# Which queue sends the key bits: seven dictionary and set entries of a hash-attention and SwiGLU kernel

## The chip, the cores and the metric

The kernel runs on one core of a Trainium2 chip. The metric is the device time of one execution in microseconds. Before the change three executions took 327.55, 328.31 and 328.44 us, a median of 328.31 us. One more execution was profiled; the views quoted below are of that one.

## The reference, cut to what matters

The first stage is attention over buckets: six sign bits of a projection give every query and key a bucket number, and a query sees only the keys of its own bucket. The second stage is a SwiGLU layer with RMS norm over the rows that the attention gives.

```
B, H, S, D = 4, 8, 768, 64                      # q, k, v; proj is 64 x 6
q_bits = einsum(q, proj) > 0 ; k_bits = einsum(k, proj) > 0
mask   = bucket(q_bits) == bucket(k_bits)       # bucket = sum of bits * 2^i
attn   = softmax(where(mask, q k^T / 8, -1e9))  # divided by (sum + 1e-9)
x      = (attn v) as 3072 rows of 512
xn     = x / sqrt(mean(x^2) + 1e-6) * rms_g
out    = (silu(xn w_gate) * (xn w_val)) w_out   # 512 -> 1536 -> 512
```

## The kernel before, in words

**Units and steps.** The work is cut into eight units. Unit `u` is one half (384) of the query rows of batch `u // 2`, for all eight heads. A unit has `NS` = 24 steps, three for each head, and a step handles 256 of the 768 keys. The main loop (L916 to L921) does for every step `t`: the scores of step `t + 1` on PE (`scores`, L359), the exponential of step `t` on ACT (`probs`, L371), and then what `plan[t]` holds, in the order in which it was put there with `at(0, t, ...)`. The order of each engine and of each DMA queue is thus written out by hand; nothing reorders it later. Each queue issues in order, and an issue that must wait holds all that stand behind it.

**Bits in the operands.** For each pair of heads `hp` of batch `b` a tile of `qks` (six of them, used in turn, L80) holds q and k transposed in its rows 0 to 63. Rows 64 to 69 hold the six bits as fp16 values of equal size and either sign, so that one matmul gives q k^T plus a large bonus for a full match. For the pairs of `spots` (L714) the bits come about so: `hash_one` projects on PE (L222) when the step in `spots[..][3]` comes, `hash_bits` takes the signs on DVE (L231), and `send_bits` (L306, issue at L312) carries them to the rows of the operand tile with four small DMAs for each head (two for k, two for q; 4.5 KB each). `SENDS` (L809) gives the step of a head's four DMAs where it differs from the hash step; `ONPOOL` (L812) names the heads whose DMAs are issued from GpSimd's queue (POOL) and not from SyncE's (SP). `place` (L814) puts both into a list `late`, which is put into the plan behind everything that the units themselves planned (L884).

**Loads.** `spots` also says at which step a pair's raw q and k blocks are loaded (`load_blocks`, L116: four DMAs for q, four for k, in runs of 128 bytes) and its values (`load_v`, L107: one DMA of 384 KB, or two of 192 KB for pairs in `VSPLIT`, L105). For pair (2, 0) the entry is a triple: k blocks, q blocks, values. All loads share the eight buffers of `lpool` and go out on SP. `turn_dve` transposes blocks on DVE (L192, L199), `cast_pool` writes them into the operand tile from POOL (L212), `v_prep` and `v_sum` copy and sum the values on POOL (L321, L328 to L330).

**A unit's second stage.** While unit `u + 1` does its attention, unit `u` goes through norm and feed-forward. At step 4 of that stretch `norm` (L457) runs: DVE adds up the squares (L422, L450), POOL takes the power -1/2 (`rstd`, L454), DVE scales the rows (`xn`, L463 and L471). One step later `turn_dma` (L439) transposes the 128-row thirds named by `ONDMA` with DMA transposes from SP (L442): two thirds in units 1 to 4 and 6, three in unit 5, one in unit 7. The other thirds go through PE, with the result taken up by DVE (L478, L484). During steps 0 to some 8 PE finishes the output projection of the unit before (`project`, L524; `store`, L534, copies on ACT at L536 and stores 256 KB from SP at L537, one step later than the last matmul). The gate and value matmuls (L495, `g_ps` and `v_ps`) follow and need all thirds of `xnT`.

The places that the change touches are thus steps 53 and 54 (norm and transposes of unit 1), steps 62 (loads), and steps 97 to 101 (norm of unit 3 at step 100, transposes at 101).

Of the kernel before, what the change touches and what calls it, by code (L numbers as in the profile page):

```python
# [33 lines left out]
def kernel(  # L34
# [67 lines left out]
        )  # L102


    VSPLIT = {(2, 3), (3, 0), (3, 1), (3, 2), (3, 3)}  # L105

    def load_v(eng, b, hp):  # L107
        vn = lpool.tile([128, 2, 6, D], FP32, name="vn", tag="L")
        for hs in (slice(0, 1), slice(1, 2)) if (b, hp) in VSPLIT else (slice(0, 2),):
            eng.dma_start(  # L110
# [587 lines left out]
    for hp, ts in ((0, (8, 22, 23, 24, 25, 24, 39, 27, 28, 42)), (1, (20, 26, 28, 29, 30, 29, 41, 32, 33, 43))):  # L698
# [15 lines left out]
    spots = {  # L714
# [91 lines left out]
            inserts[2 * b * NS + s] = (MEAN, v_mean, b, hp, 4)  # L806


    SENDS = {(1, 2, 0): 54, (1, 2, 1): 54, (2, 0, 0): 77, (2, 0, 1): 77, (2, 2, 1): 101, (3, 2, 1): 149}  # L809


    ONPOOL = {(1, 2, 0), (1, 2, 1)}  # L812

    def place(t, step):  # L814
        if step[0] is None:
# [2 lines left out]
        if step[0] is hash_one:  # L818
            late.append((t, hash_bits, *step[1:]))
            for pair in step[1:]:  # L820
                for hh in range(2):
                    s = SENDS.get((*pair, hh), t)
                    eng = nc.gpsimd if (*pair, hh) in ONPOOL else nc.sync
                    late.append((max(s, t), send_bits, *pair, hh, eng))
# [150 lines left out]
```

## Time and profile before

| what | us |
|---|---|
| three runs: lowest, median, highest | 327.55, 328.31, 328.44 |
| the profiled execution's own time | 328.73 |
| its span, first to last instruction | 326.9 |
| PE busy, of the span | 320.4 |
| VectorE (DVE) / ScalarE (ACT) / GpSimd (POOL) busy | 227.5 / 228.4 / 160.4 |
| granted TensorE clock | 1.000 |

Times in the views count from the start of the span. A row of the timeline gives start, duration, engine, line of the kernel, instruction, result and operands, how many were merged into the row (x4), and in square brackets how long the engine had been idle before it and who released it. "SPq" is the queue of SyncE, on which most DMAs are issued: the duration there is that of issuing, not of the transfer. "PEld" is TensorE's weight load.

### The profile page before, as it was taken

The numbers are of one execution on the slowest core, as the hardware profiler recorded it, in microseconds if no ns is written. First come the engines' busy times: TensorE is split into PE (matmuls) and PEld (weight loads), VectorE is DVE, ScalarE is ACT, GpSimd is POOL, SyncE is SP. The second block draws the span as 40 slices with busy tenths as digits, with TensorE's granted clock in tenths as the row PEclk, the third lists the DMA queues.
The fourth block names the chain that finished last, engine by engine and source line by source line (L and its number), as shares of the span: only waits on it lengthen the run. The fifth ranks groups of instructions, "written<-read, shape, count | busy, mean of one in ns | idle before, by whom it ended". The sixth has DMA issues, their size and how long they took to land.

```text
span 326.9 us, 7765 instructions
## 1 busy us (share of the span) xinstructions
PE 320.4 (98%) x2943; PEld 194.0 (59%) x2943; DVE 227.5 (70%) x510; ACT 228.4 (70%) x333; POOL 160.4 (49%) x211
## 2 busy tenths in 40 slices
PE   9999999999999999999899999999999999999996
PEld 4576666655566565655466556665656556665554
DVE  5887876866888568874689558787567536773870
ACT  6899987677678676777667768686777768754322
POOL 3999849957967363731873522742582111221000
PEclk9999999999999999999999999999999999999999
DMA  7953999984728863056547047001300040002002
GB/s 231 357 173 91 223 214 199 172 172 82 167 35 158 153 141 87 7 90 127 108 110 146 34 106 138 7 6 52 99 6 3 1 99 32 2 2 96 17 2 96
DMA packets 87613, 33.03 MB, mean 101 GB/s; under 512 B 72780, under 2 KB 84504, under 8 KB 87576
## 3 DMA queue, kind: packets, MB, share of 16 engines
q1 hardware_dynamic: 83416, 27.71, 36.3%
q0 software_dynamic: 3936, 4.76, 8.7%
q8 instruction: 23, 0.38, 0.5%
q14 instruction: 14, 0.11, 0.1%
q10 hardware_dynamic: 224, 0.07, 0.1%
HBM read 28.58 MB, written 6.29 MB: 107 GB/s over the span
## 4 chain that ended last, share of the span: by engine, by line
PE 94%; DMA 2%; DVE 1%; ACT 1%; SPq 0%; issue 0%; POOL 0%
PE g_ps L495 19%; PE v_ps L495 19%; PE s_ps L359 19%; PE y_ps L524 16%; PE o_ps L384 10%; PE t_ps L160 2%; PE d_ps L222 2%; DMA xnT<-xn 2%; PE d_ps L242 2%; PE z_ps L591 1%; PE y_ps L543 1%; ACT psb L371 1%; PE x_ps L478 1%; PE m_ps L343 1%; SPq L442 0%; DVE xn L463 0%
## 5 line engine op out<-in xcount | busy, mean ns | idle before, releaser
L371 ACT ACTIVATE psb<-s_ps,ebias 128x768 f16<-128x768 f32 x192 | 167.9, 900 | 18.3 <-PE s_ps L359 17.1
L359 PE MATMUL s_ps<-QK 128*128 128x384 f16 (+1 forms) x384 | 93.5, 326 | 1.2 <-ACT psb L371 1.1
L503 ACT ACTIVATE t<-g_ps 128x384 f32<-128x384 f32 x96 | 47.2, 492 | 55.6 <-PE g_ps L495 53.4
L495 PE MATMUL g_ps<-xnT,wg 128*128 128x384 f16 x384 | 82.5, 326 | 1.8 <-DMA xnT<-xn 1.7
L495 PE MATMUL v_ps<-xnT,wv 128*128 128x384 f16 x384 | 82.0, 326 | 0.0
L512 DVE SCALAR_TENSOR_TENSOR a<-t,g_ps 128x384 f32<-128x384 f32 x96 | 52.9, 551 | 33.1 <-ACT t L503 31.6
L406 POOL TENSOR_TENSOR x<-otmp,rcp 128x384 f32<-128x384 f32 x29 | 24.3, 838 | 91.3 <-DVE rcp L404 91.1
L524 PE MATMUL y_ps<-wo,ht 128*128 128x512 f16 x276 | 67.5, 379 | 0.0
L513 DVE SCALAR_TENSOR_TENSOR ht<-a,v_ps 128x384 f16<-128x384 f32 x96 | 53.2, 554 | 11.5 <-PE v_ps L495 3.6
L384 PEld LDWEIGHTS <-psb 128*128 128x128 f16 x1152 | 52.0, 97 | 15.1 <-issue 0.6
L384 PE MATMUL o_ps<-vl,psb 128*128 128x65 f16 x1152 | 55.8, 193 | 0.0
L359 PEld LDWEIGHTS <-QK 128*128 128x128 f16 (+1 forms) x384 | 34.7, 98 | 33.8 <-issue 8.6
L495 PEld LDWEIGHTS <-wg 128*128 128x128 f16 x384 | 35.1, 97 | 23.5 <-issue 2.7
L495 PEld LDWEIGHTS <-wv 128*128 128x128 f16 x384 | 35.1, 97 | 20.8 <-issue 0.2
L524 PEld LDWEIGHTS <-ht 128*128 128x128 f16 x276 | 24.9, 98 | 23.2
L399 DVE TENSOR_TENSOR otmp<-o_ps,cvb 128x390 f32<-128x390 f32 x32 | 17.8, 557 | 9.2 <-PE o_ps L384 9.2
L536 ACT COPY ysb<-y_ps 128x512 f32<-128x512 f32 x23 | 13.5, 587 | 15.0 <-PE y_ps L524 15.0
L412 POOL TENSOR_TENSOR sq<-x 128x384 f32<-128x384 f32 x24 | 19.9, 827 | 1.9
L212 POOL CAST QK<-qT 64x768 f16<-64x768 f32 x20 | 16.4, 821 | 8.3 <-DVE qT L199 7.6
L212 POOL CAST QK<-kT 64x768 f16<-64x768 f32 x20 | 16.4, 821 | 7.7 <-DVE kT L199 5.7
L199 DVE STREAM_TRANSPOSE kT<-kL 128x192 f32<-128x192 f32 x32 | 16.6, 520 | 0.0
L199 DVE STREAM_TRANSPOSE qT<-qL 128x192 f32<-128x192 f32 x32 | 16.1, 523 | 0.0
(86 smaller groups left out, 268.1 us busy)
## 6 DMA issues: line engine op xcount, KB each, us to landing
out_dram<-ysb SPq DMA_DIRECT2D x23, 256.0 KB
vn<-in_v_dram SPq DMA_DIRECT2D x11, 384.0 KB
qL<-in_q_dram SPq DMA_DIRECT2D x40, 96.0 KB
kL<-in_k_dram SPq DMA_DIRECT2D x40, 96.0 KB
kn<-in_k_dram SPq DMA_DIRECT2D x5, 384.0 KB
qn<-in_q_dram SPq DMA_DIRECT2D x5, 384.0 KB
vn<-in_v_dram SPq DMA_DIRECT2D x10, 192.0 KB
wg<-in_moe_w_gate_dram POOLq DMA_DIRECT2D x2, 768.0 KB, 8.8
```

Of the source, the lines that this page charges most:

```text
L199: nc.vector.transpose(dst.rearrange("p (c t r) -> p r c t", c=6, r=4)[:, r], src.rearrange("p (r c) d -> p r c d", r=4)[:, r],)
L212: nc.gpsimd.tensor_copy(QK[b, 2 * hp + hh, "h"][0:64, o : o + S], src[64 * hh : 64 * hh + 64, :])
L359: nc.tensor.matmul(ps[:, j, 0:HALF], QK[b, h, "h"][rows, S + jt * 128 : S + (jt + 1) * 128], QK[b, h, "h"][rows, half * HALF : (half + 1) ...
L371: nc.scalar.activation(psb[u, h][:, 2 * ch : 2 * ch + 2, :], sps.pop((u, i))[:, :, 0:HALF], AF.Exp, bias=ebias, scale=ESCALE,)
L384: nc.tensor.matmul(o[:, c, hh, 0:65], psb[u, h][:, jt, c * 128 : (c + 1) * 128], vls[b % 2][:, h, 2 * (jt % 3) + jt // 3 if b in PARITY el ...
L406: eng.tensor_mul(xd.rearrange("p c (h d) -> p c h d", h=2), tmp[:, :, :, 0:64], r.to_broadcast([128, 3, 2, 64]),)
L412: eng.tensor_mul(sq, xd, xd)
L495: nc.tensor.matmul(ps, w[:, kt, fs], xnT[u][:, kt, :], start=(kt == 0), stop=(kt == 3))
L503: nc.scalar.activation(t, fbank[u, ft, "g_ps"], AF.Tanh, scale=0.5)
L512: nc.vector.scalar_tensor_tensor(out=a, in0=t, scalar=1.0, in1=g, op0=ALU.add, op1=ALU.mult)
L513: nc.vector.scalar_tensor_tensor(out=ht[u][:, ft, :], in0=a, scalar=0.5, in1=vv, op0=ALU.mult, op1=ALU.mult)
L524: nc.tensor.matmul(y, ht[u][:, ft, c * 128 : (c + 1) * 128], wo[:, ft, :], start=(ft == 0), stop=(ft == NF - 1),)
```

## The change

Seven entries change; no function does.

- `VSPLIT` keeps only pair (3, 3): the values of (2, 3), (3, 0), (3, 1) and (3, 2) are loaded by one DMA each and no longer by two.
- Pair (2, 0): its k and q blocks are loaded at step 54 (before: 53), and its values at step 62 (before: 54).
- Batch 1's third pair, second head (1, 2, 1): its four bit DMAs go out at step 53 on SP, behind the transposing DMAs of unit 1. Before they went out at step 54 on POOL, behind those of the first head, which stay there.
- Batch 2's third pair (2, 2): the bit DMAs of both heads go out on POOL at step 101, behind the power of unit 3's norm. Before they went out on SP: those of the first head at step 97, ahead of unit 3's transposing DMAs, and those of the second at step 101, behind them.

```diff
-    VSPLIT = {(2, 3), (3, 0), (3, 1), (3, 2), (3, 3)}
+    VSPLIT = {(3, 3)}
...
-        (2, 0): ((53, 53, 54), (63, 64, 65, 66), (67, 69, 70, 71), 73),
+        (2, 0): ((54, 54, 62), (63, 64, 65, 66), (67, 69, 70, 71), 73),
...
-    SENDS = {(1, 2, 0): 54, (1, 2, 1): 54, (2, 0, 0): 77, (2, 0, 1): 77, (2, 2, 1): 101, (3, 2, 1): 149}
+    SENDS = {(1, 2, 0): 54, (1, 2, 1): 53, (2, 0, 0): 77, (2, 0, 1): 77, (2, 2, 0): 101, (2, 2, 1): 101, (3, 2, 1): 149}
...
-    ONPOOL = {(1, 2, 0), (1, 2, 1)}
+    ONPOOL = {(1, 2, 0), (2, 2, 0), (2, 2, 1)}
```

The instructions of PE, DVE and ACT and their order are the same in both kernels. SP's queue around unit 1 reads after the change: transposes x2, bits of (1, 2, 1) x4, a store, k blocks x4, q blocks x4, a store, bits of (1, 3) x8, values of (2, 0), blocks of (2, 1). Before it read: transposes x2, k blocks x4, q blocks x4, a store, values of (2, 0), a store, bits of (1, 3) x8, blocks of (2, 1). Around unit 3 it reads after the change: values of (3, 0), a store, transposes x2, a store, blocks of (3, 1). Before: values of (3, 0) x2, bits x4, a store, transposes x2, bits x4, a store, blocks of (3, 1).

## Prediction

> **What bounds the kernel now.** I read the page's busy line first, then PE's waits, then PE's timeline where it waits, and last SP's queue in front of those places.
>
> ```profile
> PE 320.4 (98%) x2943; PEld 194.0 (59%) x2943; DVE 227.5 (70%) x510; ACT 228.4 (70%) x333; POOL 160.4 (49%) x211
> PE g_ps L495 <- DMA xnT<-xn: 1.7, 2, 1.5
> PE s_ps L359 <- ACT psb L371: 1.1, 2, 0.8
> 79.51 0.48 PE L495 MATMUL g_ps<-xnT,wg 128*128 128x384 f16 x2 [0.27 <-DMA xnT<-xn]
> 153.94 1.03 PE L524 MATMUL y_ps<-wo,ht 128*128 128x512 f16 x4
> 156.44 0.48 PE L495 MATMUL g_ps<-xnT,wg 128*128 128x384 f16 x2 [1.47 <-DMA xnT<-xn]
> ```
>
> PE is busy in 320.4 of 326.9 us, and the change leaves its instructions as they are. So it can win only what PE waits, and lose by new waits. PE waits twice for the DMA transposes: 0.27 us before unit 1's first gate matmul and 1.47 us before unit 3's. Together 1.74 us; that is all there is to win, since the change touches nothing that ACT's two waits hang on. The row at 153.94 says when PE ran out of work: 153.94 + 1.03 = 154.97, and 156.44 - 1.47 says the same.
>
> Now what holds the transposes, on SP, DVE and ACT:
>
> ```profile
> 74.22 1.42 DVE L463 SCALAR_TENSOR_TENSOR xn<-x,rstd,grow 128x512 f16<-128x512 f32 x2 [1.00 <-POOL rstd L454]
> 75.00 2.63 SPq L442 DMA_TRANSPOSE xnT<-xn  x2
> ...
> 146.22 1.06 SPq L110 DMA_DIRECT2D vn<-in_v_dram  x2
> 147.38 3.03 SPq L312 DMA_DIRECT2D QK<-bits  x4
> 150.52 0.38 SPq L537 DMA_DIRECT2D out_dram<-ysb  x1
> 151.00 2.59 SPq L442 DMA_TRANSPOSE xnT<-xn  x2
> 146.45 0.59 ACT L536 COPY ysb<-y_ps 128x512 f32<-128x512 f32 x1 [1.10 <-PE y_ps L524]
> 148.57 1.41 DVE L463 SCALAR_TENSOR_TENSOR xn<-x,rstd,grow 128x512 f16<-128x512 f32 x2 [0.97 <-POOL rstd L454]
> ```
>
> In unit 1 SP is idle and issues the first transpose 75.00 - 74.22 = 0.78 us after DVE has begun on `xn`: the data sets the time. In unit 3 it is 151.00 - 148.57 = 2.43 us. There SP is the one that is late: four bit DMAs (3.03 us, 0.76 each) and a store lie ahead.
>
> **Unit 3, part by part.** The four bit DMAs go from ahead of the transposes to POOL. The values need one issue and not two; one takes 0.59 us (row at 107.91, below), so SP is free at 146.81. The store's data is ready when ACT's copy ends, 146.45 + 0.59 = 147.04; its 0.38 us ends by about 147.5, before `xn` exists. So the first transpose goes out at 148.57 + 0.78 = 149.35, 1.65 us earlier. How long from there to the matmul? Four units show it:
>
> ```profile
> 111.06 3.71 SPq L442 DMA_TRANSPOSE xnT<-xn  x2
> 116.39 0.49 PE L495 MATMUL g_ps<-xnT,wg 128*128 128x384 f16 x2
> 117.36 0.81 PE L495 MATMUL v_ps<-xnT,wv 128*128 128x384 f16 x4
> 189.70 2.57 SPq L442 DMA_TRANSPOSE xnT<-xn  x2
> 193.64 0.81 PE L495 MATMUL g_ps<-xnT,wg 128*128 128x384 f16 x4
> ```
>
> Unit 1: 79.51 - 75.00 = 4.51, PE waiting. Unit 3: 156.44 - 151.00 = 5.44, PE waiting. Units 2 and 4 didn't wait, so the data was there in at most 5.33 and 3.94. Unit 1 is the nearest, since eight of POOL's bit DMAs ran beside it, as they will now in unit 3. 149.35 + 4.51 = 153.86; with the worst, 149.35 + 5.44 = 154.79. Both are before 154.97. So the whole 1.47 us goes, with 1.1 to 0.2 us of cover left. What is late next: `v_ps` needs the bank that ACT's copy of the last `y_ps` frees, at 155.01 + 0.59 = 155.60 (row below); unit 2 shows `v_ps` 0.97 us behind `g_ps`, so it is due at 155.94. No wait.
>
> **The bits on POOL.**
>
> ```profile
> 73.30 0.88 POOL L454 TENSOR_TENSOR rstd<-ss,mhalf 128x3 f32<-128x3 f32 x1 [1.71 <-DVE ss L450]
> 74.15 4.09 POOL L312 DMA_DIRECT2D QK<-bits  x8
> 147.68 0.86 POOL L454 TENSOR_TENSOR rstd<-ss,mhalf 128x3 f32<-128x3 f32 x1 [1.04 <-DVE ss L450]
> 155.01 0.83 POOL L406 TENSOR_TENSOR x<-otmp,rcp 128x384 f32<-128x384 f32 x1 [6.48 <-DVE rcp L404]
> QK<-bits POOLq DMA_DIRECT2D x8, 4.5 KB, 1.9
> 155.01 0.59 ACT L536 COPY ysb<-y_ps 128x512 f32<-128x512 f32 x1 [0.17 <-PE y_ps L524]
> 158.38 0.49 PE L359 MATMUL s_ps<-QK 128*128 128x384 f16 x2
> 159.96 0.49 PE L359 MATMUL s_ps<-QK 128*128 128x384 f16 x2
> ```
>
> Eight issues took 4.09 us (0.51 each) in unit 1. In unit 3 they start behind the power, 147.68 + 0.86 = 148.54, and end at 152.63. Queued behind them on POOL is L406, which waits for DVE until 155.01: 2.4 us of cover. With 1.9 us from issue to landing the first head's bits are there at 148.54 + 2.05 + 1.9 = 152.5, the second's at 154.5. Their readers are the scores of unit 4's heads 4 and 5: the first is step 108, 159.96 now and 158.49 after the gain, the second three steps of about 1.6 us later. 6 us of cover; cost zero. DVE's `xn` took 1.42 us beside POOL's issues and 1.41 without them, so DVE isn't slowed.
>
> Here a page speaks against the change. The Trainium skill, "SBUF — State Buffer", section "SBUF: two separate sides", says that a DMA issued from GpSimd can't get its descriptors written while VectorE runs in a mode that takes both ports; its part "A bandwidth-pool intuition that's wrong (but worth ruling out)" gives about 620 ns alone and 3100 ns beside such an operation. By it eight issues could take some 20 us (an estimate from that page's ratio), and the change would lose. The trace of unit 1, 0.51 us each beside `xn`, doesn't bear this out.
>
> **Unit 1.** Four of POOL's eight bit DMAs leave; the four that stay end at 74.15 + 2.05 = 76.2, before the second transpose is issued (L442's second half, about 76.4). So unit 1 comes near unit 4, which had none: 75.00 + 3.94 = 78.94 at the latest, against 79.51 - 0.27 = 79.24 where PE needs it. I take the full 0.27; the bounds are 0 and 0.27.
>
> What moves on SP behind the transposes:
>
> ```profile
> 77.72 2.69 SPq L125 DMA_DIRECT2D kL<-in_k_dram  x4
> 88.86 6.00 SPq L312 DMA_DIRECT2D QK<-bits  x8
> 97.67 3.65 SPq L125 DMA_DIRECT2D kL<-in_k_dram  x4
> 107.91 0.59 SPq L110 DMA_DIRECT2D vn<-in_v_dram  x1
> 108.75 0.37 SPq L537 DMA_DIRECT2D out_dram<-ysb  x1
> 88.03 0.50 PE L359 MATMUL s_ps<-QK 128*128 128x384 f16 x2
> 91.26 0.53 DVE L199 STREAM_TRANSPOSE kT<-kL 128x192 f32<-128x192 f32 x1
> 105.40 0.51 DVE L199 STREAM_TRANSPOSE kT<-kL 128x192 f32<-128x192 f32 x1
> 118.28 0.83 POOL L321 CAST vl<-vn 128x768 f16<-128x768 f32 x1
> 100.00:101.00 1.00, 1.00 (x8) 0.59 (x6) 0.86 (x4) 0.66 (x2) 0.48 (x1) 1.00 0.21 31
> 110.00:112.00 2.00, 2.00 (x19) 1.10 (x18) 1.76 (x3) 1.38 (x2) 0.21 (x1) 1.00 0.83 298
> ```
>
> Four bit issues (6.00 / 8 = 0.75 each, 3.0 us) and one store (0.4) come ahead of pair (2, 0)'s blocks. The bits are issued by 80.7 and land by 82.6; unit 2's head 5 reads them at 88.03. The k blocks go out 3.5 us later, by 83.9, the q blocks by 86.7, the last store by 87.1; DVE first turns k at 91.26. Pair (1, 3)'s bits wait for DVE until 88.86 as before, with 1.7 us of room on SP. The values of (2, 0) now follow those bits and are read at 118.28. All hidden.
>
> They push the blocks of (2, 1) and (2, 2), though, by one issue, 0.59 us: the k blocks of (2, 1) are issued by 101.9 for a turn at 105.40; unit 2's store ends on SP at 109.7, and its transposes start at 111.06, still set by DVE. On SP this costs nothing. On the DMA engines 384 KB more have to go through between 95 and 112 us; the slice at 100 has a share of 0.21 only, so most of it fits. I take zero; the upper bound is the transfer itself, 384 KB (393,216 bytes) at the 298 GB/s of the last row, 1.3 us, all of it in front of unit 2's transposes.
>
> **The single value loads** save SP 1.06 - 0.59 = 0.47 us four times. Nothing reads half of such a load, and only the first, before unit 3's transposes, stands near a wait; it is counted above. Behind unit 3's transposes SP has eight bit issues less, so all later loads go earlier: zero.
>
> **The sum.** 1.47 + 0.27 = 1.74 us off the profiled execution's 328.73 (326.9 span and 1.83 around it): 326.99. That execution is 0.42 above the median of the three runs; from the median 328.31 the same sum gives 326.6, which I forecast.
>
> **The rivals.**
>
> *A: DMA traffic, not SP's order, makes unit 3 late.* For it: from issue to matmul unit 3 took 0.93 us longer than unit 1, and between 153 and 156 us an instruction fetch ran among the transposes' packets:
>
> ```profile
> q8 instruction: 1, 0.02, 3.1%
> ```
>
> 3.1% of 16 engines in 3 us is 1.49 us on one engine. (The Trainium skill, "Runtime: NRT & Kernel Launch", "Instruction fetch mechanics", calls such a refill mostly hidden; by that A would be empty. The row shows only that one was there.) With the fetch and POOL's DMAs both against it the time is 5.44 + (4.51 - 3.94) = 6.01, so 155.36, a wait of 0.39. If the transposes gain nothing by the earlier issue, the 1.47 stays and only unit 1's 0.27 goes: 328.04 from the median. That is also the case where the change doesn't do what it says.
>
> *B: unit 2 pays.* Its transposes were there in at most 5.33 us, and how much sooner isn't shown. If the moved values delay them by the full 1.3 us and nothing covers it: 328.31 - 1.74 + 1.3 = 327.9. Against it: the idle slice at 100, and that SP itself is in time.
>
> *C, slower: POOL's issues are slow beside DVE.* It decides when the first head's four DMAs take over 158.49 - 1.9 - 148.54 = 8.05 us, 2.0 each instead of 0.51. Priced by POOL's longest operation near here,
>
> ```profile
> 102.31 2.65 POOL L150 MEMSET QK<- 64x3072 f16 x1
> ```
>
> 2.65 each: head 4's bits at 161.0, PE waits 2.5; head 5's at 171.6, needed at 163.3 + 2.5, another 5.8. 328.31 - 1.74 + 8.3 = 334.9. Unit 1's row speaks against it.
>
> **How the numbers follow.** Forecast 0.68, A 0.12, B 0.12, C 0.08. About 0.3% (1.0 us) is what a measurement here can tell from no change. The forecast is faster by 0.53%; A and B stay within 0.3%; C is slower. The forecast's own range is 326.57 less or plus the runs' scatter (0.76 below the median, 0.13 above) and 0.5 for a small rest of wait: 325.9 to 327.2. To take in A and B the range goes to 328.2; C is left out.
>
> **What would show it.** Right: no wait of PE for `xnT` in units 1 and 3; unit 3's first L442 0.8 us behind `xn`; eight L312 on POOL in about 4 us behind the power. Wrong: L442 at its old distance, or a landing over 5.6 us behind it (A); a wait of `g_ps` in unit 2 (B); L406 or the scores of unit 4's heads 4 and 5 waiting for bits (C).

## The result, and the profile after

| | median, us | lowest to highest | runs |
|---|---|---|---|
| before | 328.14 | 327.55 to 328.46 | 6 |
| after | 326.12 | 325.67 to 326.49 | 6 |

The ratio is 0.994, with a 95% interval of 0.9927 to 0.9953: 2.02 us less. The profiled execution of the changed kernel took 326.49 us, with a span of 324.7 us at a granted clock of 1.000; that of before took 328.73. The same kernel was timed once more beside the experiments (`after_again`, below): 326.15 against 328.09.

The busy line of the page after, and the rows of PE's waits (us in total, times, longest):

```profile
PE 319.9 (99%) x2943; PEld 194.2 (60%) x2943; DVE 227.6 (70%) x510; ACT 228.4 (70%) x333; POOL 162.4 (50%) x215
PE s_ps L359 <- ACT psb L371: 1.1, 2, 0.8
PE z_ps L591 <- PEq L959: 0.8, 1, 0.8
```

The row for `xnT` is gone from the list of waits. What is left stands before 28 us of the span (0.77 at the start, 0.76 at 10.33 and 0.39 at 27.50 us), and nothing of the change reaches it. Next, PE's timeline after, at the gate matmuls of units 1 and 3:

```profile
77.97 1.03 PE L524 MATMUL y_ps<-wo,ht 128*128 128x512 f16 x4
78.84 0.49 PE L495 MATMUL g_ps<-xnT,wg 128*128 128x384 f16 x2
...
153.32 1.02 PE L524 MATMUL y_ps<-wo,ht 128*128 128x512 f16 x4
154.18 0.49 PE L495 MATMUL g_ps<-xnT,wg 128*128 128x384 f16 x2
```

No square bracket stands behind either `g_ps`. There is a better measure of what went than the bracket: the distance from the last `y_ps` group to `g_ps`. In unit 3 it was 156.44 - 153.94 = 2.50 us and is now 154.18 - 153.32 = 0.86: 1.64 us, where the bracket said 1.47. For unit 1 the row of before is this:

```profile
78.21 1.02 PE L524 MATMUL y_ps<-wo,ht 128*128 128x512 f16 x4
```

79.51 - 78.21 = 1.30 became 78.84 - 77.97 = 0.87: 0.43 us, where the bracket said 0.27. Both times the bracket is 0.16 to 0.17 us short. It counts from the end of the last matmul, and without a wait the next group starts before that end. Comparing the start of each step's scores in the two traces, the kernel after is 0.2 us ahead 31 us into the span, where nothing of the change reaches; the shift then changes by 0.44 us at step 58 and by 1.62 at step 106, and nowhere else by more than some 0.04.

The two prices together are 2.07 us, near the measured 2.02. That they fit so closely is in part luck: the profiled execution of before took 328.73 us, 0.59 more than the median of 328.14, and its wait in unit 3 was the longest that any trace shows (below).

The queues around unit 3 after the change, SP and then DVE and POOL:

```profile
145.36 0.59 SPq L110 DMA_DIRECT2D vn<-in_v_dram  x1
146.43 0.36 SPq L537 DMA_DIRECT2D out_dram<-ysb  x1
148.76 2.55 SPq L442 DMA_TRANSPOSE xnT<-xn  x2
...
147.95 1.42 DVE L463 SCALAR_TENSOR_TENSOR xn<-x,rstd,grow 128x512 f16<-128x512 f32 x2 [0.97 <-POOL rstd L454]
147.05 0.86 POOL L454 TENSOR_TENSOR rstd<-ss,mhalf 128x3 f32<-128x3 f32 x1 [1.05 <-DVE ss L450]
147.87 4.06 POOL L312 DMA_DIRECT2D QK<-bits  x8
154.39 0.83 POOL L406 TENSOR_TENSOR x<-otmp,rcp 128x384 f32<-128x384 f32 x1 [2.46 <-DVE rcp L404]
```

SP is done with the store at 146.79 and issues the first transpose 148.76 - 147.95 = 0.81 us behind `xn`, where it was 2.43. POOL's eight issues fit between the power and L406, which still waits 2.46 us for DVE.

### The profile page after: what moved, and what is told of

Same layout as the page of the kernel before. It is cut to its first block, busy times and chain, and to the rows that moved or that the text cites. A ratio compares the mean times of both kernels' runs of the same rounds, so it can differ in the third digit from the quotient of the medians.

```text
span 324.7 us, 7758 instructions
## 1 busy us (share of the span) xinstructions
PE 319.9 (99%) x2943; PEld 194.2 (60%) x2943; DVE 227.6 (70%) x510; ACT 228.4 (70%) x333; POOL 162.4 (50%) x215
## 4 chain that ended last, share of the span: by engine, by line
PE 98%; ACT 1%; issue 0%
PE s_ps L359 20%; PE g_ps L495 19%; PE v_ps L495 19%; PE y_ps L524 18%; PE o_ps L384 11%; PE t_ps L160 2%; PE d_ps L222 2%; PE d_ps L242 2%; PE z_ps L591 1%; PE y_ps L543 1%; PE x_ps L478 1%; PE m_ps L343 1%; ACT psb L371 1%; PE s_ps L160 0%; ACT ypart L548 0%
## 5 line engine op out<-in xcount | busy, mean ns | idle before, releaser
L371 ACT ACTIVATE psb<-s_ps,ebias 128x768 f16<-128x768 f32 x192 | 167.9, 900 | 18.4 <-PE s_ps L359 17.3
L406 POOL TENSOR_TENSOR x<-otmp,rcp 128x384 f32<-128x384 f32 x29 | 24.3, 837 | 89.2 <-DVE rcp L404 88.9
```

Of the source, the lines that this page charges most:

```text
L371: nc.scalar.activation(psb[u, h][:, 2 * ch : 2 * ch + 2, :], sps.pop((u, i))[:, :, 0:HALF], AF.Exp, bias=ebias, scale=ESCALE,)
L406: eng.tensor_mul(xd.rearrange("p c (h d) -> p c h d", h=2), tmp[:, :, :, 0:64], r.to_broadcast([128, 3, 2, 64]),)
```

## The experiments

Two theories were to be told apart for unit 3. **Q**, that of the prediction: SP's order makes the transposes late. **F**, the prediction's rival A: what runs on the DMA engines beside the transposes, an instruction fetch above all, makes them land late. For unit 1: **P**, eight of POOL's bit DMAs beside the transposes cost 0.27 us and four don't, against **L**, the block loads behind the transposes cost it. All kernels are edits of the kernel before unless they are said to start from the one after. "Before" is each time the kernel before on the same chip.

### Unit 3's part alone

```diff
-    SENDS = {..., (2, 2, 1): 101, ...}
+    SENDS = {..., (2, 2, 0): 101, (2, 2, 1): 101, ...}
-    ONPOOL = {(1, 2, 0), (1, 2, 1)}
+    ONPOOL = {(1, 2, 0), (1, 2, 1), (2, 2, 0), (2, 2, 1)}
```

> Only the bits of pair (2, 2) go to POOL behind unit 3's power; everything else as before. Queue theory (SP's four bit DMAs ahead of unit 3's transposes are the cause): PE's 1.47 us wait in unit 3 goes and the 0.27 us in unit 1 stays. Between the same two matmul groups PE needed 2.50 us with the wait and 0.86 without (before and after), so the price is 1.64 and not 1.47: about 326.5 against 328.14. Traffic rival (DMA traffic and an instruction fetch make the landing late, whatever SP does): the wait stays near 1.5 and the time at 328.1. Rival that the gain came from several edits together: under half, over 327.3.

326.68 us (11 runs, 326.1 to 327.11) against 327.93: ratio 0.9966 (0.9954 to 0.9977), 0.75 to 1.5 us less. Unit 3's wait is gone and unit 1's stays (`g_ps` for `xnT`: 0.3 us, once). This is the greater part of the change.

### Unit 1's part alone, twice

```diff
-        (2, 0): ((53, 53, 54), ...
+        (2, 0): ((54, 54, 62), ...
-    SENDS = {..., (1, 2, 1): 54, ...}
+    SENDS = {..., (1, 2, 1): 53, ...}
-    ONPOOL = {(1, 2, 0), (1, 2, 1)}
+    ONPOOL = {(1, 2, 0)}
```

> Only unit 1's part: bits of (1, 2, 1) on SP at step 53, blocks of (2, 0) at 54, its values at 62. Queue theory: the wait of 0.27 in unit 1 goes, worth 0.27 plus some 0.16 of matmul tail, 0.43; the wait in unit 3 stays at 1.47. Time 327.7. Rival (the moved loads cost something later, in unit 2): a new wait of up to 1.3 us there, time 328.1 to 329.

> Unit 1's whole part again, since it gave 0.07 us where its trace shows 0.43 less in unit 1. If the first result was scatter: 0.3 to 0.5 below before. If something takes the 0.43 back: level with before again, and unit 3's wait, or another, is longer by 0.4.

327.85 (11 runs) against 327.93, ratio 0.9998 (0.9987 to 1.0009), and again 327.65 (11 runs) against 327.96, ratio 0.9993 (0.9984 to 1.0002). In both traces unit 1's wait is gone and the step there is 0.43 to 0.44 us shorter, but the timed gain, 0.1 and 0.3 us, can't be told from nothing. The first of the two, unit 1 and unit 3 (PE):

```profile
78.26 1.02 PE L524 MATMUL y_ps<-wo,ht 128*128 128x512 f16 x4
79.12 0.49 PE L495 MATMUL g_ps<-xnT,wg 128*128 128x384 f16 x2
...
153.57 1.03 PE L524 MATMUL y_ps<-wo,ht 128*128 128x512 f16 x4
155.68 0.49 PE L495 MATMUL g_ps<-xnT,wg 128*128 128x384 f16 x2 [1.08 <-DMA xnT<-xn]
```

Unit 3, which this kernel doesn't touch, waits 1.08 us here and 1.17 in the other run, where the profiled execution of before had 1.47. So the length of that wait differs between traces that have the same order around unit 3, and the one profiled of before was on the long side. By the distance between the groups it cost 155.68 - 153.57 - 0.86 = 1.25 us here, which is what unit 3's part alone gave (327.93 - 326.68).

### The same without the later loads

Only the bits of (1, 2, 1) go to SP at 53; the blocks and values of (2, 0) stay where they were.

```diff
-    SENDS = {..., (1, 2, 1): 54, ...}
+    SENDS = {..., (1, 2, 1): 53, ...}
-    ONPOOL = {(1, 2, 0), (1, 2, 1)}
+    ONPOOL = {(1, 2, 0)}
```

> Of unit 1's part only the bits: the four of (1, 2, 1) go out on SP at step 53, behind the transposes; the blocks and values of (2, 0) stay at their steps. Theory P (four POOL bit DMAs less beside the transposes free them): the wait of 0.27 in unit 1 goes. Rival L (the block loads that followed the transposes at once were in the way): they still follow, only 3 us later, so it goes here too; the next kernel tells P and L apart. Time at most 0.43 us less, 327.6 to 328.1; the wait in unit 3 stays at 1.1 to 1.5.

Slower: 329.73 (7 runs, 328.33 to 331.83) against 327.96, ratio 1.005 (1.0026 to 1.0074). The profiled execution is one of the shorter ones (328.70). Its PE, DVE and SP rows, and then the DMA share (the number before the last; the last is GB/s) in this kernel and in the one after:

```profile
78.48 0.49 PE L495 MATMUL g_ps<-xnT,wg 128*128 128x384 f16 x2
92.66 0.48 PE L359 MATMUL s_ps<-QK 128*128 128x384 f16 x2 [1.04 <-DMA QK<-bits]
...
87.26 0.55 DVE L231 TENSOR_SCALAR bits<-d_ps 128x384 uint16<-128x384 uint16 x1
...
86.65 0.58 SPq L537 DMA_DIRECT2D out_dram<-ysb  x1
87.29 0.42 SPq L110 DMA_DIRECT2D vn<-in_v_dram  x1
87.81 0.45 SPq L537 DMA_DIRECT2D out_dram<-ysb  x1
88.36 5.96 SPq L312 DMA_DIRECT2D QK<-bits  x8
...
90.00:92.00 2.00, 1.62 (x18) 0.86 (x15) 1.79 (x5) 1.91 (x3) 1.92 (x3) 1.00 0.57 213
```

```profile
90.00:92.00 2.00, 2.00 (x21) 1.14 (x20) 1.81 (x4) 1.66 (x4) 1.84 (x4) 1.00 0.04 11
```

Unit 1's wait is gone, but the bits of pair (1, 3) now land too late and PE waits 1.04 us for them. Two things add up. First, SP is late: two stores (512 KB) and the values (384 KB) stand just ahead of the bits in its queue, and it issues the bits 88.36 - 87.26 = 1.10 us after DVE has begun on them, where it took 0.58 us before the change and 0.57 after it: 0.52 us late. Second, the bits take longer once issued: the reader starts 92.66 - 88.36 = 4.30 us behind the first issue, where in the kernel before the same reader started 92.60 - 88.86 = 3.74 us behind it and didn't wait, so they land at least 0.56 us later. From 90 to 92 us, where the DMA engines were nearly idle in the kernel after (0.04), they are at 0.57. So the later loads aren't a detail of the change; they keep SP and the DMA engines free for those bits. Whether the later values or the store that comes out ahead of the later blocks does more of it wasn't separated.

### Only the later loads

```diff
-        (2, 0): ((53, 53, 54), ...
+        (2, 0): ((54, 54, 62), ...
```

> Of unit 1's part only the loads of (2, 0): blocks at step 54, values at 62; all eight bits of (1, 2) stay on POOL. A store of 256 KB now follows the transposes on SP, and the blocks come behind it. Theory P: the wait in unit 1 stays at 0.2 to 0.3. Rival L: it goes. Time 328.0, within 0.4.

327.58 (11 runs) against 327.96, ratio 0.9997 (0.9987 to 1.0006). Unit 1's wait is there as before, though the first block is now issued behind a store:

```profile
73.37 4.09 POOL L312 DMA_DIRECT2D QK<-bits  x8
74.22 2.63 SPq L442 DMA_TRANSPOSE xnT<-xn  x2
76.94 0.53 SPq L537 DMA_DIRECT2D out_dram<-ysb  x1
77.56 2.74 SPq L125 DMA_DIRECT2D kL<-in_k_dram  x4
78.70 0.48 PE L495 MATMUL g_ps<-xnT,wg 128*128 128x384 f16 x2 [0.25 <-DMA xnT<-xn]
```

From the issue to `g_ps` it takes 78.70 - 74.22 = 4.48 us, as in before (4.51), and in the kernel above, with the loads unmoved and four DMAs on POOL, at most 78.48 - 74.41 = 4.07 (its L442 starts at 74.41). P holds. L falls for the block loads. In this kernel, though, a store follows the transposes at once, so another bulk transfer could stand in the blocks' place. Unit 4 of before speaks against that: a store follows its transposes (issued at 189.70) at once as well,

```profile
192.36 1.67 SPq L537 DMA_DIRECT2D out_dram<-ysb  x2
```

and without bit DMAs of POOL its data was there in at most 3.94 us.

### Both heads on SP, behind the transposes

```diff
-    SENDS = {..., (2, 2, 1): 101, ...}
+    SENDS = {..., (2, 2, 0): 101, (2, 2, 1): 101, ...}
```

> The bits of both heads of (2, 2) stay on SP, but all eight behind unit 3's transposes; nothing else changed. Queue theory: only the order on SP matters, POOL isn't needed: L442 starts 0.8 us behind xn, no wait in unit 3, 326.5. The eight issues then end some 6 us after the transposes, near 158, and land near 160; head 4's scores are due at 158.4 and its four DMAs land near 157. Rival (SP can't afford eight issues there): scores of unit 4's head 4 or 5 wait, up to 1 us, or the loads of (3, 1) come late; then 326.9 to 328.

327.46 (12 runs) against 327.93, ratio 0.9988 (0.9978 to 0.9999): less than half of what POOL's queue gives. SP and PE here:

```profile
148.88 2.55 SPq L442 DMA_TRANSPOSE xnT<-xn  x2
151.52 5.99 SPq L312 DMA_DIRECT2D QK<-bits  x8
...
165.56 6.00 SPq L312 DMA_DIRECT2D QK<-bits  x8
...
153.43 1.03 PE L524 MATMUL y_ps<-wo,ht 128*128 128x512 f16 x4
154.29 0.49 PE L495 MATMUL g_ps<-xnT,wg 128*128 128x384 f16 x2
...
168.32 0.48 PE L359 MATMUL s_ps<-QK 128*128 128x384 f16 x2 [0.71 <-DMA QK<-bits]
```

Order alone takes unit 3's wait away. What POOL's queue adds is room on SP: with all sixteen bit issues on it, those of pair (2, 3) start at 165.56, not at 161.98 as in the kernel after, and PE waits 0.71 us for them. How much of that is SP and how much the landing wasn't separated: the DMA engines are at 0.97 from 164 to 166 us. In the kernel before, the bits of (2, 3) start at 164.95 and their reader at 169.70, 4.75 us behind them and not 2.76 as here: there unit 3's own wait puts PE back.

### After, with the first head's bits back ahead of the transposes

```diff
-    SENDS = {..., (2, 2, 0): 101, (2, 2, 1): 101, ...}      # from the kernel after
-    ONPOOL = {(1, 2, 0), (2, 2, 0), (2, 2, 1)}
+    SENDS = {..., (2, 2, 1): 101, ...}
+    ONPOOL = {(1, 2, 0), (2, 2, 1)}
```

> The changed kernel with one thing undone: the first head of (2, 2) is back on SP at step 97, ahead of unit 3's transposes; the second stays on POOL. Queue theory: L442 is again held to some 2 us behind xn and the wait of about 1.5 us comes back; 327.8. If the value load in one issue saves 0.47 us on SP as counted, L442 starts 0.5 us earlier than before and the wait is about 1.0 (327.3). Traffic rival: no wait, 326.1, since four of the bits are on POOL and fewer small DMAs follow the transposes on SP.

327.4 (10 runs) against 327.93, ratio 0.9986 (0.9976 to 0.9995). The wait is back, 0.80 us by its bracket, at 154.59, with L442 issued at 148.94 behind four bit issues and a store, 1.55 us behind `xn` (147.39). The first head's place on SP is what counts, not the second's queue.

### The single value loads, alone and taken out of the change

```diff
-    VSPLIT = {(2, 3), (3, 0), (3, 1), (3, 2), (3, 3)}
+    VSPLIT = {(3, 3)}
```

> Only the single value loads, everything else as before. They free 0.47 us on SP before unit 3's transposes, so L442 there starts 0.5 us sooner, at about 150.5. Theory one: the wait in unit 3 shrinks by that, to 1.0; 327.5. Theory two, an instruction fetch near 153.3 sets the landing: the transposes land when the fetch lets them, and the wait doesn't shrink; 327.9. In no case a gain behind unit 3.

327.85 (11 runs) against 328.09, ratio 0.9994 (0.9986 to 1.0003). The reverse, from the kernel after:

> The changed kernel with the values again in two DMAs for pairs (2, 3), (3, 0), (3, 1), (3, 2). The bits of (2, 2) on POOL alone gave 1.25 us and unit 1's part alone nothing that can be measured, which leaves 0.7 of the 2.0 us. Theory one: the waits' prices (1.64 and 0.43) hold and the rest is scatter; the single value loads are worth nothing, 326.1. Theory two: the rest comes from the single value loads (0.47 us of SP's time each): 326.8.

326.43 (5 runs) against 328.09, ratio 0.9948 (0.9936 to 0.996), beside 326.15 (6 runs), ratio 0.9947 (0.9934 to 0.996), for the unedited kernel after in the same runs:

> The changed kernel again, beside the next three. 326.1 as measured, 1.8 to 2.0 below before.

So single loads are worth nothing that shows. But the first of these says more about unit 3:

```profile
150.16 2.58 SPq L442 DMA_TRANSPOSE xnT<-xn  x2
153.43 1.03 PE L524 MATMUL y_ps<-wo,ht 128*128 128x512 f16 x4
155.53 0.50 PE L495 MATMUL g_ps<-xnT,wg 128*128 128x384 f16 x2 [1.07 <-DMA xnT<-xn]
```

From issue to `g_ps` it is 155.53 - 150.16 = 5.37 us, as long as in before (5.44) and 0.9 longer than unit 1's 4.5, with nothing of POOL's beside it. POOL's bit DMAs don't explain that length, and the place in SP's queue only sets when it begins.

### The instruction fetch moved

An instruction fetch is here a packet of the DMA queue that the page calls `instruction`: q8 has 23 of them with 0.38 MB in the execution before, some 16 KB each. It runs on the same DMA engines as the data; the one in unit 3 takes 18.4% of 16 engines over half a microsecond (row in "Where the fetch lies"), which is 1.47 us on a single engine.

Ninety tiny matmuls (8 columns) are added at the start of the kernel; their result is unused. SP's order stays that of before. They push the later instructions of PE further back in its stream, so that a fetch falls on another moment.

```diff
+    for _ in range(90):
+        nc.tensor.matmul(wz[:, 0:8], ones_sq, ones_row[:, 0:8], start=True, stop=True)
```

> The kernel before with 90 tiny matmuls (8 columns, result unused) behind the six idle ones at its start. They add 180 instructions to PE, so the 16 KB instruction fetches come at other points: near unit 3 some 9 us earlier and 5 us later than now, none beside the transposes. The time as a whole grows by the tiny matmuls and isn't the measure; the wait in unit 3 is. Queue theory alone: L442 still starts 2.4 us behind xn and the wait is 1.5 as before. Fetch theory: the transposes land 3.9 to 4.5 us behind the first L442, and the wait falls to 0.0 to 0.6.

One execution, 330.89 us, of which the added matmuls take their part; only the places count here. Unit 3, and then unit 5:

```profile
150.90 1.41 DVE L463 SCALAR_TENSOR_TENSOR xn<-x,rstd,grow 128x512 f16<-128x512 f32 x2 [0.97 <-POOL rstd L454]
149.59 3.01 SPq L312 DMA_DIRECT2D QK<-bits  x4
153.18 2.57 SPq L442 DMA_TRANSPOSE xnT<-xn  x2
156.27 1.03 PE L524 MATMUL y_ps<-wo,ht 128*128 128x512 f16 x4
157.16 0.48 PE L495 MATMUL g_ps<-xnT,wg 128*128 128x384 f16 x2
...
227.28 4.79 SPq L442 DMA_TRANSPOSE xnT<-xn  x3
233.45 0.81 PE L495 MATMUL g_ps<-xnT,wg 128*128 128x384 f16 x4 [0.39 <-DMA xnT<-xn]
```

In unit 3 the transposes go out 153.18 - 150.90 = 2.28 us behind `xn`, behind four bit issues as in before, and PE doesn't wait: the data is there 157.16 - 153.18 = 3.98 us after the issue at the latest. In that stretch the DMA view has no line for an instruction queue; its bulk is this one:

```profile
q1 hardware_dynamic: 1244, 0.53, 52.2%
```

In unit 5 a fetch now falls beside the transposes (a row of 1.7% from 228 to 233 us), their issue takes 4.79 us and not 3.86, and PE waits 0.39 us where it hadn't. A new wait of 0.74 us stands in unit 7 at 302.46, again with a fetch beside the transpose (2.1% from 298 to 302.4). Unit 1's wait is as before (0.27). Q alone forecast 1.5 us for unit 3. So in unit 3 of before both hold: the issue is late *and* the fetch holds up the transposes. With the issue as late but no fetch beside it PE doesn't wait here, and in the kernels with the early issue the fetch begins too late to hold it up.

Units 5 and 7 add something that isn't in either theory: there the issue is on time (0.77 and 0.82 us behind `xn`, as before), and PE waits beside a fetch all the same. A late issue isn't needed where the cover is thin.

### After, with the fetch among the transposes again

From the kernel after, with five such matmuls (result unused).

```diff
+    for _ in range(5):
+        nc.tensor.matmul(wz[:, 0:8], ones_sq, ones_row[:, 0:8], start=True, stop=True)
```

> The changed kernel with 5 tiny matmuls (8 columns, result unused) at its start: 10 instructions more on PE, so every 16 KB instruction fetch comes some 0.5 us earlier against the work, in unit 3 onto the end of the second transpose. SP's order is that of the changed kernel. Fetch theory: the transposes become visible some 1.5 us behind the fetch's end, so about 0.3 to 0.6 us late: a wait of that size in unit 3. Queue theory: no wait in unit 3, 1.5 us of cover.

One execution, 325.92 us, no wait in unit 3. But it missed its aim: the fetch started in the half microsecond from 151.67, 3.5 to 4.0 us behind the first issue (148.17), as in the kernel after. For unit 3 it says nothing of a fetch that hits.

## Where the fetch lies, in all kernels

The DMA view, cut to half microseconds from the first issue in unit 3, shows in which of them the fetch started. The row of before, 153.0 to 153.5, and that of after, 152.26 to 152.76:

```profile
q8 instruction: 1, 0.02, 18.4%
```

```profile
q8 instruction: 1, 0.02, 22.1%
```

| kernel | fetch starts behind the first issue, us | issue to `g_ps`, us | wait shown, us |
|---|---|---|---|
| before | 2.0 to 2.5 | 5.44 | 1.47 |
| later loads alone | 2.0 to 2.5 | 5.15 | 0.92 |
| unit 1's part, twice | 2.5 to 3.0 | 5.42, 5.24 | 1.08, 1.17 |
| bits of (1, 2, 1) alone | 2.5 to 3.0 | 5.20 | 1.12 |
| single value loads alone | 2.5 to 3.0 | 5.37 | 1.07 |
| after, first head back on SP | 3.0 to 3.5 | 5.65 | 0.80 |
| after, unit 3's part, both on SP behind | 3.5 to 4.0 | at most 5.42 | none |
| fetch moved | none | at most 3.98 | none |

All columns are of unit 3. Where PE waited, the third column is the landing; where it didn't, the data was there earlier by an unknown amount. With a fetch beginning 2.0 to 3.5 us behind the issue the transposes take 5.15 to 5.65 us; without one at most 3.98 to 4.07, or 4.5 beside eight of POOL's DMAs. The fetch hardly moves with the change (it begins near 153.3 us before and near 152.5 after), while the transposes go out 2.24 us earlier, so that it starts 3.5 to 4.0 us behind their issue and PE doesn't wait.

## Why the prediction was right, step by step

- **All there is to win is PE's two waits: right.** Both went, and nothing else moved that the change reaches. The size was too small: 1.47 and 0.27 are brackets, and in the two profiled executions the prices are 1.64 and 0.43. That is 0.33 us of the 0.45 between the forecast before rounding (326.57) and the measured 326.12; another 0.17 is that more runs of before gave 328.14, not 328.31. The two make 0.50, and the rest is within the scatter. How near the number came is partly luck: the prediction took 1.47 us from an execution 0.42 us above its median and subtracted it from the median, and the four other traces that leave unit 3's order alone (unit 1's part twice, its bits alone, its loads alone) lose 1.08 to 1.33 us there, by the distance between the groups, and not 1.64. A wait that was too long for the median made up for a bracket that is too short.
- **Unit 3, SP free in time, L442 0.78 us behind `xn`: right,** 0.81.
- **Landing 4.51 to 5.44 us later: the outcome right, the reason incomplete.** The prediction took 4.51 from unit 1, since POOL's DMAs would run in unit 3 as they did there, and 5.44 as the worst. Most of the spread goes with the fetch. With it, 5.15 to 5.65 us from the issue at 148.76 end at 153.91 to 154.41, and PE needs the data at 154.18: of the predicted cover of 1.1 to 0.2 us, something between 0.27 us of cover and a wait of 0.23 would be left if the fetch fell among the packets. It began too late for that, which the prediction hadn't worked out: it gave this case, POOL's DMAs included, a wait of 0.39 us under rival A. Whether a wait would come back in unit 3 with the early issue isn't shown; units 5 and 7 of "The instruction fetch moved" show that it can elsewhere.
- **POOL's eight issues of 0.51 us behind the power, DVE not slowed: right,** 4.06 us and 1.42 us for `xn`. L406 waits for DVE 2.46 us as computed (2.4). The landing took 2.0 us in the median, near the 1.9 assumed, but 4.0 for the slowest of the eight; the 6 us of cover took that in. No bits are waited for, so rival C fell. The slow descriptor writes that the Trainium skill, "SBUF — State Buffer", section "SBUF: two separate sides", describes don't show in these issues; no run shows whether `xn` runs in the mode that it means, so its rule is not tested here.
- **Unit 1 comes near unit 4: right,** at most 4.08 us from issue to `g_ps`, where unit 4 has at most 3.94; the four DMAs on POOL are the cause ("The same without the later loads" and "Only the later loads"). What of its 0.43 us reaches the timed runs of that part alone isn't settled.
- **What moves on SP is hidden: right, by less than was said.** The prediction left 1.7 us of room ahead of pair (1, 3)'s bits. These are SP's rows after:

```profile
74.76 2.63 SPq L442 DMA_TRANSPOSE xnT<-xn  x2
77.49 2.96 SPq L312 DMA_DIRECT2D QK<-bits  x4
80.55 0.38 SPq L537 DMA_DIRECT2D out_dram<-ysb  x1
81.03 3.52 SPq L125 DMA_DIRECT2D kL<-in_k_dram  x4
84.66 2.65 SPq L125 DMA_DIRECT2D qL<-in_q_dram  x4
87.41 0.58 SPq L537 DMA_DIRECT2D out_dram<-ysb  x1
88.19 5.97 SPq L312 DMA_DIRECT2D QK<-bits  x8
```

  SP is free at 87.99, 0.20 us ahead of the bits: the k blocks took 3.52 us to issue, not 2.69, and PE's gain brought the bits forward to 88.19. Room on SP is also only half of what there was to count. The kernel with the loads unmoved has none (its bits go out 0.52 us late), and at least as much again, 0.56 us, was lost in the landing.
- **Moved values cost unit 2 nothing: right.** Unit 2 doesn't wait (rival B).
- **Single value loads are worth zero: right,** twice.
- **Rival A** was priced as if DMA traffic and SP's order excluded each other. In unit 3 of before the wait took both, so it fell as a forecast and holds as a mechanism.
- **The range:** 326.57 - 0.76 is 325.8 and not 325.9. Nothing hangs on it.

The sum of the parts: unit 3 alone 0.75 to 1.5 us, unit 1 alone -0.3 to 0.4 (first run) and -0.1 to 0.5 (second), the whole 1.5 to 2.4 in the first timing. The intervals allow for a plain sum, but the middles (1.1 and 0.1 to 0.3, against 2.0) leave 0.6 to 0.8 us open. The traces close part of it: unit 3's price of 1.08 to 1.33 us and unit 1's 0.43 make 1.5 to 1.8, so 0.2 to 0.5 us of the 2.0 have no cause that is shown. No kernel that was run is faster than the changed one by more than the scatter (the 325.92 with five added matmuls is one execution, inside the changed kernel's 325.67 to 326.49).

## What to carry to other kernels

Price a wait on TensorE by the distance between the groups around it, against the same place where nothing waits, and not by the idle time in the bracket. When a DMA takes longer in one place than in others, look at what shares its moment, instruction fetches included, ahead of calling it late: a wait may take both a late issue and such a neighbour, and then removing one of them can be enough, until the neighbour moves to a place with little cover. Small DMAs behind bulk can be late twice, in the issue and in the landing, so count room on the DMA engines and on the issuing queue; and compare the issue with the engine that makes the data, not with the clock of another kernel's trace. A wait that is to be subtracted from a median should not be read from one execution alone.

## What the runs showed of the hardware

- One instruction fetch that starts 2.0 to 3.5 us behind the issue of two DMA transposes of 128x512 fp16 goes with a landing about 1.1 to 1.6 us later (5.15 to 5.65 us, against at most 4.07). With 90 matmuls added the fetch was gone from there and so was the delay, and waits stood beside it in units 5 and 7 (0.39 and 0.74 us; one execution).
- Where the fetch falls into the issue itself, the issue is longer: 3.71 us for two transposes in unit 2 of before (a row of the fetch from 111.56 to 112.06 us) against 2.55 in the same unit of the kernel with 90 added matmuls, where the fetch starts 4.5 us behind the issue or later, and 4.79 against 3.86 for three in unit 5.
- Eight bit DMAs of 4.5 KB behind 896 KB of two stores and of values were issued 0.52 us late and landed at least 0.56 us later than without; PE waited 1.04 us.
- An idle bracket ahead of a matmul group was 0.16 to 0.17 us shorter than what the wait cost, in both places.
